# A delta-rule recurrence followed by an MLP: six-chunk key and query rings, a new load order, Newton key norms and a folded beta

## The chip, the cores and the metric

The kernel runs on 1 core of one Trainium2 chip. The metric is the device time of one execution in microseconds, the median over the runs of the kernel. A profile is one execution; its span is the time from the first to the last instruction of the core.

## What is computed

```python
def _attn_ref(q, k, v, beta):           # q, k, v: (4, 8, 768, 48); beta: (4, 8, 768)
    k_n = k / (np.linalg.norm(k, axis=-1, keepdims=True) + 1e-06)
    state = np.zeros((B, H, D, D))
    for t in range(S):
        y[:, :, t] = einsum('bhd,bhde->bhe', q[:, :, t], state)
        v_old = einsum('bhde,bhd->bhe', state, k_n[:, :, t])
        state = state + beta_t * einsum('bhd,bhe->bhde', k_n[:, :, t], v[:, :, t] - v_old)

def reference(...):                      # y as (3072, 384) rows x
    return gelu_tanh(x @ w_in) @ w_out   # w_in (384, 2048), w_out (2048, 384)
```

## The kernel before, in words

The sequence of 768 steps is cut into 12 chunks of C = 64 steps, for 32 heads held as 16 pairs (two heads of a pair on the two partition halves). A chunk goes through four stages.

- `prep(c)`: keys, queries and values come from DRAM by `load` (L522), two DMAs each, one for each half: 64 partitions x 16 pairs x 48 float32, 196,608 bytes a DMA. The key norms: squares `sq` on POOL or ACT, their sums `ss` (a DVE reduce, L613), the root `sr` (ACT Sqrt for chunks 0 to 2, for the later nine a POOL power with exponent 0.5, L330), an added 1e-6 (L622) and a reciprocal `rn` (L624) on DVE. Then `Kn = kf * rn` (POOL) and `Qn` (a cast), both bfloat16, and their transposes into `KQT`: on PE for chunks 0 to 2, by DMA transposes on the SP queue (L353) for the later ones. `kf`, `qf`, `vf` are rings of three buffers, `Kn` and `KQT` rings of RB = 4, indexed by chunk.
- `blocks(u)`: chunks are taken in units, [0], [1,2], [3,4], ..., [9,10], [11]. For a unit the 16x16 diagonal blocks of all its triangular systems are solved at once: matmuls of `own(u)` fill PSUM, a DVE 32x32 transpose makes `Tt` (L740), a product with `bM` makes `Yf`, then 14 pairs of small elementwise steps `tmp`, `Yf` run on POOL (on DVE for unit 0), and `XW[1]` (POOL, times minus beta) and `XW[0]` (ACT, a copy) go back to PE. All POOL work stands in one in-order queue, with the weight loads that POOL issues.
- `inverse(c, hs)`: from the solved blocks the whole 64x64 inverse `TT` of the chunk, by DVE products with masks (`WB` and `DI`, 128x1024 from PSUM, L785; `ET`; three `TT` steps) between PE products; `gram(c, g)` gives `G` and the masked `DT`.
- `state(c)`: the serial chain over chunks. `R = v - K S` (DVE), PE product with `TT`, `U = beta * (...)` (DVE, a product with `bcol`), PE product with `Kn`, `S = S + ...` (DVE), and the chunk's output `x` (ACT). The product of `U` and `Kn` is the last reader of `Kn`.

`mlp(t)` follows for tiles of one or two chunks, [0], [1,2], ..., [9,10], [11]: `x` is rearranged by six small DMAs on the SP queue, 16 groups of three matmuls `ps<-x,W` each followed by a Gelu on ACT into `gT`, then groups of eight matmuls `ps<-W,gT`, a copy `osb` and a store.

What sets the order: `Plan` holds every operation with a cost, its dependencies and a priority; `schedule()` (L106) places them one after another, per engine the ready operation with the lowest priority among those that are not later than `NEAR` of that engine, and emits each engine's queue in that fixed order with semaphore waits. Priorities are `T(c) = 28 c`; `prep(c)` has T(c-1), the MLP T + 1000 so that it fills gaps, its x DMAs a very low value. Loads are a queue of their own in one respect: `gate()` (L519) makes each load wait for the landing of the load written two before it in the program (`bulk[-2]`), and W_in (`load_w1`, `load_w1x`, eight DMAs) and W_out (`load_w2`, four DMAs) take part in it, issued by POOL. An instruction that waits holds back everything behind it on its queue. The plan's costs are estimates written into the kernel (1.05 us of DMA time for one key, query or value DMA); the chip's times are in the trace.

The program order of the loads is kf0, beta, qf0, kf1, qf1, vf0, W_in, kf2, qf2, vf1, W_out, vf2, then from iteration c = 1 on kf, qf and vf of chunk c + 2, each followed by `prep(c + 2)`:

```python
for c in range(NCH):
    if c + 2 < NCH:
        if c > 0:
            load("kf", c + 2, T(c - 1))
            load("qf", c + 2, T(c - 1))
        load("vf", c + 2, T(c - 1))
        prep(c + 2)
    u, sl = unit_of(c)
    if c == UNITS[u][0]:
        hs = blocks(u)
        ...
    state(c)
```

Of the kernel before, what the change touches and what calls it, by code (L numbers as in the profile page):

```python
# [376 lines left out]
def bass_deltanet__then__act_gelu_tanh_kernel(  # L377
# [25 lines left out]
    with nc.allow_non_contiguous_dma("head rows"), nc.allow_low_precision("bf16 matmuls"):  # L403
# [194 lines left out]

        def prep(c):
            s, i, j = c % RL, c % RB, c % 2  # L600
            pr = T(c, -STEP)
# [13 lines left out]
            ssn = [f"ss{j}{n}" for n in range(len(parts))]  # L615
            if c < NPE:
                op({"act": 0.24}, {"act": f_act(sr[j][:, :], ss[j][:, :], ACT.Sqrt)},
                   reads=ssn, writes=[f"sr{j}"], prio=pr)
            else:
                op({"pool": 2.95}, {"pool": f_tt(sr[j][:, :], ss[j][:, :], half[:, :], ALU.pow)},  # L620
                   reads=ssn + ["half"], writes=[f"sr{j}"], prio=pr)
            op({"dve": 0.1}, {"dve": lambda e: e.tensor_scalar(ss[j][:, :], sr[j][:, :], 1e-6, None, op0=ALU.add)},  # L622
               reads=[f"sr{j}"], writes=ssn, prio=pr)
            op({"dve": 0.25}, {"dve": lambda e: e.reciprocal(rn[j][:, :], ss[j][:, :])},  # L624
               reads=ssn, writes=[f"rn{j}"], prio=pr)
# [415 lines left out]
```

## Time and profile before

| | |
|---|---|
| median of 3 runs | 319.52 us (318.8 to 319.82) |
| the profiled execution | 316.87 us, its span 315.1 us |
| mean granted clock of PE over the span | 0.836 |
| PE busy | 240.2 us (76%) |
| DVE busy | 159.9 us (51%) |
| POOL busy | 139.8 us (44%) |
| ACT busy | 123.5 us (39%) |

PE is TensorE's matmuls, PEld its weight loads, DVE VectorE, ACT ScalarE, POOL GpSimd, SP the queue that issues most DMAs. In lines of the trace, `L330 POOL TENSOR_TENSOR sr<-ss,half 128x16` is an operation at line 330 (a helper's line, so tiles name the operation) that writes `sr` from `ss` and `half`; in square brackets, or behind a bar, stands the idle time before it and what ended it.

### The profile page before, as it was taken

What the parts mean: (1) busy time and instruction counts of PE and PEld (TensorE: products, weight loads), DVE (VectorE), ACT (ScalarE), POOL (GpSimd) and SP (SyncE); (2) the same over time, 40 slices, a digit from 0 to 9 for tenths busy, and PEclk for the clock granted to TensorE, in tenths of its full rate; (3) what the DMA queues carried; (4) which work ended last, traced back from release to release, by engine and by line L of the source; (5) the groups of instructions that cost most, each with busy time, mean ns of one, the idle gap of its engine ahead of it and who ended that gap; (6) DMA issues with size and microseconds to landing.
All of it is one profiled execution on the core that took longest, in us unless ns stands there. A gap on an engine that the chain in (4) does not pass through costs nothing.

```text
span 315.1 us, 13554 instructions
## 1 busy us (share of the span) xinstructions
PE 240.2 (76%) x6289; PEld 153.0 (49%) x6310; DVE 159.9 (51%) x250; ACT 123.5 (39%) x209; POOL 139.8 (44%) x246
## 2 busy tenths in 40 slices
PE   1714671779746869974897985899897999989995
PEld 1513660346644315664754553346665556455662
DVE  5799650119765212988633652347775545252111
ACT  3622460642213464221263742473122752166240
POOL 4580368572555499940103794995100006810000
PEclk9955555779755799985587999799998899999999
DMA  7999895999991985103299849800351000200112
GB/s 126 149 151 127 124 142 94 160 147 158 146 127 24 151 117 111 54 29 57 57 165 128 158 70 151 180 2 4 46 121 42 3 4 27 89 4 2 58 50 50
DMA packets 102808, 28.40 MB, mean 90 GB/s; under 512 B 96768, under 2 KB 102368, under 8 KB 102752
## 3 DMA queue, kind: packets, MB, share of 16 engines
q1 hardware_dynamic: 100128, 24.39, 48.0%
q0 software_dynamic: 2624, 3.15, 7.1%
q8 instruction: 49, 0.80, 1.1%
q14 instruction: 7, 0.06, 0.1%
HBM read 20.64 MB, written 4.72 MB: 80 GB/s over the span
## 4 chain that ended last, share of the span: by engine, by line
PE 38%; DMA 25%; SPq 14%; DVE 7%; ACT 6%; POOL 5%; issue 5%
PE ps L346 38%; DMA qf<-in_q_dram 14%; SPq L354 11%; DMA kf<-in_k_dram 3%; DMA W<-in_moe_w_out_dram 3%; DMA W<-in_moe_w_in_dram 3%; SPq L353 3%; POOL Yf L330 2%; DVE DI L785 2%; POOL tmp L330 2%; ACT gT L339 2%; ACT x L339 1%; DVE TT L330 1%; DVE U L330 1%; DVE R L330 1%
## 5 line engine op out<-in xcount | busy, mean ns | idle before, releaser
L346 PE MATMUL ps<-x,W 128*128 128x512 bf16 (+1 forms) x315 | 74.4, 379 | 18.7 <-DMA x<-x 9.7
L339 ACT ACTIVATE gT<-ps 128x512 bf16<-128x512 f32 (+1 forms) x112 | 58.2, 535 | 56.2 <-PE ps L346 54.7
L346 PE MATMUL ps<-W,gT 128*128 128x384 bf16 x384 | 69.4, 333 | 2.0 <-ACT gT L339 2.0
L346 PEld LDWEIGHTS ps<-x,W 128*128 128x128 bf16 x336 | 29.2, 104 | 51.8 <-ACT gT L339 18.9
L346 PEld LDWEIGHTS ps<-W,gT 128*128 128x128 bf16 x384 | 36.0, 99 | 26.0 <-ACT gT L339 2.6
L330 POOL TENSOR_TENSOR sr<-ss,half 128x16 f32<-128x16 f32 x9 | 26.2, 2912 | 30.8 <-DVE ss L613 30.8
L330 DVE TENSOR_TENSOR TT<-ps,DI 128x768 bf16<-128x768 f32 (+2 forms) x36 | 24.2, 688 | 18.4 <-PE ps L346 18.3
L613 DVE TENSOR_REDUCE ss<-sq 128x16 f32<-128x768 f32 (+1 forms) x13 | 11.5, 888 | 39.9 <-ACT sq L339 39.5
L330 POOL TENSOR_TENSOR Yf<-Yf,tmp 128x28 f32<-128x28 f32 (+6 forms) x84 | 28.8, 349 | 4.0
L346 PE MATMUL ps<-KQT 48*32 48x32 bf16 (+1 forms) x1280 | 22.5, 214 | 10.2 <-DMA KQT<-Kn 5.0
L330 POOL TENSOR_TENSOR tmp<-Yf 128x28 f32<-128x28 f32 (+6 forms) x84 | 27.8, 338 | 4.2
L330 POOL TENSOR_TENSOR Kn<-kf,rn 128x768 bf16<-128x768 f32 (+1 forms) x12 | 17.1, 1423 | 26.5 <-PE ps L346 22.8
L330 POOL TENSOR_TENSOR Yf<-Tt,bM 128x512 f32<-128x512 f32 x6 | 7.7, 1281 | 40.9 <-DVE Tt L740 40.9
L339 ACT ACTIVATE x<-ps 128x1024 bf16<-128x1024 f32 x12 | 12.3, 1024 | 31.8 <-PE ps L346 31.5
L346 PEld LDWEIGHTS ps<-KQT 48*32 48x32 bf16 (+1 forms) x1280 | 16.7, 106 | 16.1 <-DMA KQT<-Kn 5.9
L335 DVE COPY osb<-ps 128x384 f32<-128x384 f32 x16 | 8.9, 557 | 27.2 <-PE ps L346 26.9
L694 DVE TENSOR_TENSOR DT<-ps,mD 128x512 bf16<-128x512 f32 x24 | 16.3, 687 | 12.7 <-ACT G L339 12.3
L339 ACT ACTIVATE G<-ps 128x512 bf16<-128x512 f32 x24 | 13.9, 593 | 18.2 <-PE ps L346 18.0
L785 DVE TENSOR_TENSOR DI<-ps,mB 128x1024 bf16<-128x1024 f32 x12 | 14.6, 1219 | 11.2 <-PE ps L346 10.1
L346 PE MATMUL ps<-TT,ET 64*64 64x32 bf16 (+1 forms) x768 | 18.2, 184 | 2.5 <-DVE TT L330 1.8
L346 PEld LDWEIGHTS ps<-TT,ET 64*64 64x64 bf16 x768 | 16.2, 120 | 7.7 <-DVE TT L330 3.6
L785 DVE TENSOR_TENSOR WB<-ps,mB 128x1024 bf16<-128x1024 f32 x12 | 14.6, 1220 | 5.2 <-PE ps L346 5.2
(83 smaller groups left out, 285.8 us busy)
## 6 DMA issues: line engine op xcount, KB each, us to landing
kf<-in_k_dram SPq DMA_DIRECT2D x24, 192.0 KB, 4.8
qf<-in_q_dram SPq DMA_DIRECT2D x24, 192.0 KB, 4.8
vf<-in_v_dram SPq DMA_DIRECT2D x24, 192.0 KB, 4.4
out_dram<-osb SPq DMA_DIRECT2D x20, 192.0 KB, 2.0
W<-in_moe_w_in_dram POOLq DMA_DIRECT2D x8, 192.0 KB, 4.2
W<-in_moe_w_out_dram POOLq DMA_DIRECT2D x4, 384.0 KB, 5.3
out_dram<-osb SPq DMA_DIRECT2D x8, 96.0 KB, 2.3
x<-x SPq DMA_DIRECT2D x30, 16.0 KB, 1.9
```

The source lines that it names most:

```text
L330: return lambda e: e.tensor_tensor(out() if callable(out) else out, a() if callable(a) else a, b() if callable(b) else b, op)
L335: return lambda e: e.tensor_copy(out, a() if callable(a) else a)
L339: return lambda e: e.activation(out, a() if callable(a) else a, func)
L346: ins = t.matmul(out, lhsT, rhs, start=st, stop=sp_, skip_group_check=skip)
L353: return lambda e: e.dma_start_transpose(out, a)
L354: return lambda e: e.dma_start(out, a)
L613: op({"dve": 0.95 * w}, {"dve": lambda e, u=u: e.tensor_reduce(ss[j][:, u], sq[:, u, :], AX.X, ALU.add)}, reads=[f"sq{n}"], writes=[f"ss{j ...
L694: op(d_ps(512), {"dve": lambda e: e.tensor_tensor(pv(DTb[r_][:, ps_, :]), gview(1)(), mD[:, :].unsqueeze(1).unsqueeze(1).to_broadcast([128 ...
L785: op(d_ps(1024), {"dve": lambda e: e.tensor_tensor(dst.rearrange("q p (b j) -> q p b j", j=16), cmp_(w).unsqueeze(2).to_broadcast([128, NP ...
```

## The change

- Rings: RB goes from 4 to 6, so `Kn` and `KQT` hold six chunks. The raw rings `kf`, `qf`, `vf` stay at three.
- Loads: kf2 moves ahead of qf1, qf2 ahead of vf0 and W_in; kf3, qf3, kf4, qf4 come before W_out; vf2 after it. In the loop the key and query loads are five chunks ahead, `prep` three chunks ahead, the value load three chunks ahead and behind `state(c)`. Preps 1 and 2, and `own` and `blocks` of unit 1, get early priorities (-25.7, -25.4, -22.5, -22).
- Norms: for chunks 3 on the POOL power goes. The two chunks of a unit are normed together on DVE, from an integer estimate of the reciprocal root and three Newton steps: 13 DVE instructions on at most 128x32 for a unit (1 + 3 x 3 + 2 + a reciprocal). `Kn` of a unit's first chunk therefore waits for the keys of its second.
- Beta: `XW[0]` is multiplied by minus beta (POOL, on DVE for unit 0) in place of the ACT copy; `R` is now K S - v; `U` is then a plain copy from PSUM and goes from DVE to ACT.
- `DI` and `WB` shrink from 64 to 48 columns, so their products are 128x768. `gT` becomes a ring of 24 buffers in place of two sets of 16. The early PE transposes and Gram products may use all eight PSUM banks; the Gram product waits for `own` of its unit. `NEAR` of DVE and POOL becomes 0.1.

```diff
-NEAR = {"pe": 0.3, "dve": 0.05, "act": 0.05, "pool": 0.0, "sp": 0.0}
+NEAR = {"pe": 0.3, "dve": 0.1, "act": 0.05, "pool": 0.1, "sp": 0.0}
-        RL, RB, RT = 3, 4, 3
+        RL, RB, RT = 3, 6, 3
...
-        load("qf", 1, -66)
+        load("kf", 2, -66)
+        load("qf", 1, -65)
...
+            def norms(e, x, y):
+                return op({"dve": 0.17}, {"dve": e}, reads=x, writes=y, prio=pr)
...
+            elif c == UNITS[unit_of(c)[0]][-1]:
+                pair = UNITS[unit_of(c)[0]]
...
+                norms(lambda e: e.tensor_scalar(y_.bitcast(I32), s_.bitcast(I32), -0.5, 1597463007.0, op0=ALU.mult,
+                                                op1=ALU.add), sn_, yn_)
+                for _ in range(3):
+                    norms(f_tt(a_, y_, s_, ALU.mult), sn_ + yn_, ["nw"])
+                    norms(lambda e: e.scalar_tensor_tensor(a_, a_, -0.5, y_, ALU.mult, ALU.mult), yn_ + ["nw"], ["nw"])
+                    norms(lambda e: e.scalar_tensor_tensor(y_, a_, 1.5, y_, ALU.add, ALU.mult), yn_ + ["nw"], yn_)
+                norms(f_tt(a_, y_, s_, ALU.mult), sn_ + yn_, ["nw"])
+                norms(lambda e: e.tensor_scalar(a_, a_, 1e-6, None, op0=ALU.add), ["nw"], ["nw"])
+                op({"dve": 0.25}, {"dve": lambda e: e.reciprocal(rn2[:, z, :], a_)},
...
-                op({"pool": 2.95}, {"pool": f_tt(sr[j][:, :], ss[j][:, :], half[:, :], ALU.pow)},
...
-            op({"act": 0.65}, {"act": f_act(XW[j][0].rearrange("q c b r -> q b c r"), Y[:, :, :, :])},
+            fb = f_tt(XW[j][0].rearrange("q c b r -> q b c r"), Y[:, :, :, :],
+                      bt.unsqueeze(3).to_broadcast([128, 2, 16, 16]), ALU.mult)
+            op({"dve": 0.75} if u == 0 else {"pool": 1.5}, {"dve": fb, "pool": fb},
...
-            op(d_ps(NP * D), {"dve": f_tt(U[:, :, 0:D].rearrange("q (b m) d -> q b m d", b=2),
...
+            op(d_act(NP * D), {"act": f_act(uo, ui)}, reads=[h2] + [f"Uz{j2}"], writes=[f"U{j2}"], prio=pr)
...
+        load("qf", 2, -64)
+        load("vf", 0, -38)
         prep(0)
         prep(1)
-        load("vf", 0, -38)
...
-        load("kf", 2, -26)
-        load("qf", 2, -25)
+        prep(2)
         load("vf", 1, -24)
+        load("kf", 3, -27)
+        load("qf", 3, -26)
+        load("kf", 4, -25)
+        load("qf", 4, -24)
...
+        load("vf", 2, -15)
         for c in range(NCH):
-            if c + 2 < NCH:
-                if c > 0:
-                    load("kf", c + 2, T(c - 1))
-                    load("qf", c + 2, T(c - 1))
-                load("vf", c + 2, T(c - 1))
-                prep(c + 2)
+            if c + 3 < NCH:
+                prep(c + 3)
+            if c + 5 < NCH:
+                load("kf", c + 5, T(c - 1))
+                load("qf", c + 5, T(c - 1))
...
             state(c)
+            if c + 3 < NCH:
+                load("vf", c + 3, T(c - 1))
```

## Rows read from the trace of the kernel before

**Rows 1.** The page's 40 equal slices of the span, tenths, PE and its granted clock.
```profile
PE   1714671779746869974897985899897999989995
...
PEclk9955555779755799985587999799998899999999
```

**Rows 2.** Busy time by stretch: PE, PEld, DVE, ACT, POOL (instructions); clock, DMA share, GB/s.
```profile
5.00:45.00 40.00, 21.45 (x773) 18.01 (x777) 30.26 (x62) 17.33 (x25) 18.68 (x23) 0.65 0.96 142
54.00:103.00 49.00, 35.38 (x1072) 24.24 (x1074) 25.46 (x36) 17.62 (x35) 26.53 (x27) 0.67 0.93 127
103.00:134.00 31.00, 26.67 (x398) 13.33 (x398) 12.67 (x16) 14.63 (x25) 26.63 (x57) 0.95 0.71 107
134.00:160.00 26.00, 18.71 (x799) 15.31 (x800) 17.98 (x23) 5.86 (x9) 5.14 (x7) 0.62 0.34 60
160.00:200.00 40.00, 32.15 (x882) 18.97 (x883) 18.96 (x26) 18.36 (x30) 22.22 (x28) 0.93 0.89 138
200.00:300.00 100.00, 93.61 (x2253) 55.46 (x2264) 47.77 (x59) 43.43 (x77) 30.00 (x74) 0.98 0.15 39
```

**Rows 3.** Timeline of PE (start, duration): first MLP matmuls of tiles 0 and 1.
```profile
54.03 4.05 PE L346 MATMUL ps<-x,W 128*128 128x256 bf16 x18 [8.12 <-DMA x<-x]
...
103.25 2.34 PE L346 MATMUL ps<-x,W 128*128 128x512 bf16 x5 [0.33 <-issue]
```

**Rows 4.** Timeline of POOL: unit 1's solve and what interrupts it.
```profile
35.27 0.80 POOL L354 DMA_DIRECT2D W<-in_moe_w_out_dram  x1 [11.74 <-DMA qf<-in_q_dram]
...
42.29 1.27 POOL L330 TENSOR_TENSOR Yf<-Tt,bM 128x512 f32<-128x512 f32 x1 [1.10 <-DVE Tt L740]
...
59.76 2.94 POOL L330 TENSOR_TENSOR sr<-ss,half 128x16 f32<-128x16 f32 x1 [3.69 <-DVE ss L613]
...
65.34 1.48 POOL L330 TENSOR_TENSOR XW<-Yf,nbT 128x512 bf16<-128x512 f32 x1
```

**Rows 5.** Timeline of the SP queue: loads of qf1 and kf2.
```profile
9.25 1.31 SPq L354 DMA_DIRECT2D qf<-in_q_dram  x2
...
24.80 3.73 SPq L354 DMA_DIRECT2D kf<-in_k_dram  x2
```

**Rows 6.** Timeline of POOL: first and last operation of unit 6's solve (29 instructions between).
```profile
262.06 1.28 POOL L330 TENSOR_TENSOR Yf<-Tt,bM 128x512 f32<-128x512 f32 x1 [35.83 <-DVE Tt L740]
...
275.40 1.49 POOL L330 TENSOR_TENSOR XW<-Yf,nbT 128x512 bf16<-128x512 f32 x1
```

**Rows 7.** Waits by engine: us in total, times, longest.
```profile
ACT gT L339 <- PE ps L346: 54.7, 50, 7.5
...
POOL Kn L330 <- PE ps L346: 22.8, 5, 8.3
```

**Rows 8.** Groups of instructions by form: busy us, mean ns, idle before them.
```profile
L330 POOL TENSOR_TENSOR sr<-ss,half 128x16 f32<-128x16 f32 x9 | 26.2, 2912 | 30.8 <-DVE ss L613 30.8
...
L785 DVE TENSOR_TENSOR DI<-ps,mB 128x1024 bf16<-128x1024 f32 x12 | 14.6, 1219 | 11.2 <-PE ps L346 10.1 <-ACT TT L791 1.1
...
L330 DVE TENSOR_TENSOR U<-ps,bpad 128x768 bf16<-128x768 f32 x12 | 11.4, 952 | 11.0 <-PE ps L346 10.9
...
L330 DVE TENSOR_TENSOR ET<-ps,mE 128x768 bf16<-128x768 f32 x12 | 11.4, 951 | 2.6 <-PE ps L346 2.6
...
L330 POOL TENSOR_TENSOR XW<-Yf,nbT 128x512 bf16<-128x512 f32 x6 | 9.0, 1501 | 0.3
...
L339 ACT ACTIVATE S<-ps 128x768 bf16<-128x768 f32 x1 | 0.8, 811 | 0.2 <-PE ps L346 0.2
```

**Rows 9.** Timeline of DVE: small steps of unit 0's solve, both inputs in SBUF.
```profile
20.12 2.05 DVE L330 TENSOR_TENSOR tmp<-Yf 128x88 f32<-128x88 f32 x1
...
27.74 0.21 DVE L330 TENSOR_TENSOR tmp<-Yf 128x28 f32<-128x28 f32 x1
27.98 0.21 DVE L330 TENSOR_TENSOR Yf<-Yf,tmp 128x28 f32<-128x28 f32 x1
```

**Rows 10.** Timeline of POOL beside the first of rows 9.
```profile
20.57 1.49 POOL L330 TENSOR_TENSOR Kn<-kf,rn 128x768 bf16<-128x768 f32 x1
```

More of the change, by code (lines that the diff above doesn't have):

```diff
@@ L453, in bass_deltanet__then__act_gelu_tanh_kernel @@
         W2 = sb("W2", [128, FC, DM], BF16)
-        gT = [sb(f"gT{i}", [128, FC, 512], BF16) for i in range(2)]
+        NG = 24
+        gT = [sb(f"gT{i}", [128, 512], BF16) for i in range(NG)]
         NOSB = 4
@@ L597, in kts, with unit_of @@
             return [f"T0{c % RB}_{x}" for x in ((0, 1) if g is None else (g,))]
+        def unit_of(c):
+            return (c + 1) // 2, (c + 1) % 2
+        UNITS = [[c for c in (2 * u - 1, 2 * u) if 0 <= c < NCH] for u in range(NU)]
         def prep(c):
             s, i, j = c % RL, c % RB, c % 2
-            pr = T(c, -STEP)
+            pr = T(c, -STEP) if c in (0, 3) or c > 3 else -26 + 0.3 * c
             kn = [f"kf{s}_0", f"kf{s}_1"]
@@ L618, in prep @@
                    reads=ssn, writes=[f"sr{j}"], prio=pr)
-            else:
-                op({"pool": 2.95}, {"pool": f_tt(sr[j][:, :], ss[j][:, :], half[:, :], ALU.pow)},
[L621 to L625, printed above, removed]
+                norms(lambda e: e.tensor_scalar(sr[j][:, :], sr[j][:, :], 1e-6, None, op0=ALU.add), [f"sr{j}"], [f"sr{j}"])
@@ L626, in prep, with prep2 @@
+            for d in ([c] if c < NPE else UNITS[unit_of(c)[0]]):
+                prep2(d)
+        def prep2(c):
+            s, i, j = c % RL, c % RB, c % 2
+            pr = T(c, -STEP) if c in (0, 3) or c > 3 else -26 + 0.3 * c
+            kn = [f"kf{s}_0", f"kf{s}_1"]
+            qn = [f"qf{s}_0", f"qf{s}_1"]
+            parts = [slice(0, 8), slice(8, 16)] if c == 0 else [slice(0, NP)]
             for n, u in enumerate(parts):
@@ L659, in prep @@
                        writes=tn[kk] if np_ == 1 else [tn[kk][n]], prio=pr + 0.2 + 0.1 * kk)
-        def unit_of(c):
-            return (c + 1) // 2, (c + 1) % 2
-        UNITS = [[c for c in (2 * u - 1, 2 * u) if 0 <= c < NCH] for u in range(NU)]
         def pv(t):
@@ L823, in inverse @@
                 cols = slice(16 * k, 64)
-                op({"pe": 0.52}, {"pe": prod(hk, ET[e_], src[:, :, cols], n, per)}, nm=32, reads=sn + [f"ET{e_}"], free=[f"TT{r_}b"],
+                op({"pe": 0.52}, {"pe": prod(hk, ET[e_], src[:, :, 16 * k - off:64 - off], n, per)}, nm=32, reads=sn + [f"ET{e_}"], free=[f"TT{r_}b"],
                    writes=[hk], alloc=[(hk, NP // per)], prio=pr + 0.3 + 0.2 * k)
-                op(d_ps(16 * n), {"dve": f_tt(two(TT[r_][:, :, cols], per), view(hk, n, per), two(DI[r_][:, :, cols], per),
+                op(d_ps(16 * n), {"dve": f_tt(two(TT[r_][:, :, cols], per), view(hk, n, per), two(DI[r_][:, :, 16 * k - 16:48], per),
                                               ALU.add)},
                    reads=[hk, f"DI{r_}"], writes=[f"TT{r_}b"], prio=pr + 0.4 + 0.2 * k)
-                src, sn = TT[r_], [f"TT{r_}b"]
+                src, off, sn = TT[r_], 0, [f"TT{r_}b"]
         def state(c):
@@ L936, in mlp @@
             pr = T(chunks[-1] + 1, 1000)
-            s = t % 2
+            gs = [(16 * t + fc) % NG for fc in range(FC)]
             xs = x4[t % NX]
@@ L963, in m2 @@
                     def m2(h=h, u=u, part=part):
[L964 removed]
+                        return [(bank(h)[:, 0:DM], gT[gs[fc]][:, 128 * u:128 * u + 128], W2[:, fc, :], fc == 0,
                                  fc == FC - 1, False) for fc in range(8 * part, 8 * part + 8)]
                     op({"pe": 1.31}, {"pe": f_mms(m2)}, nm=8, mode="m", bk=mo,
[L967 removed]
+                       reads=[f"gT{gs[fc]}" for fc in range(8 * part, 8 * part + 8)] + W2N + ([h] if part else []),
                        writes=[h], alloc=[] if part else [(h, 1)], prio=pr + 40 + u * 4 + part * 2)
```

60 lines of the change are left out of this document (32 added, 28 removed).

## The prediction

> **What bounds the kernel now.** I read the page's slices first. PE is nearly full over the last third of the span and full of holes before that, at a low granted clock for most of slices 3 to 14 and again at 19 and 20 [rows 1]. So no engine bounds the whole; the kernel is PE-bound late and waits for something early. The stretches say how much: from 54 to 103 us PE is busy 35.4 of 49 us at a clock of 0.67, from 134 to 160 18.7 of 26 at 0.62, from 160 to 200 32.2 of 40, but from 200 to 300 93.6 of 100 at 0.98 [rows 2]. The MLP is the filler that would close the holes, and it can't start before its input: tile 0 begins at 54.0 us, tile 1, which needs chunks 1 and 2, only at 103.3 [rows 3]. What is late for tile 1 is the solve of unit 1 on POOL, from 42.3 to 65.34 + 1.48 = 66.8 us, with a weight issue that held POOL 11.7 us before it and a hole that ends in a root for chunk 3 within it [rows 4]. And behind that stands the load of kf2, issued at 24.8 us, 15.5 us after qf1 [rows 5]. That order of loads is what the change turns round.
>
> **The change part by part.** All times are those of the profiled execution (span 315.1).
>
> *Unit 1 starts earlier.* kf2 takes the place of qf1, 9.25 in place of 24.80 [rows 5]. With the same distance from its issue to the first step of the solve, 42.3 - 24.8 = 17.5 us [rows 4, 5], the solve starts at 26.8. Against that, kf2 and qf2 now stand ahead of vf0 and W_in: 2 x 2 x 196,608 bytes at the 142 GB/s of that stretch [rows 2] are 5.5 us of loading, and DVE, busy 30.3 of 40 us there [rows 2], is shared with unit 0's solve. So 26.8 to 32.3; I take 29, 13 us gained.
>
> *The solve itself.* It took 24.5 us. Unit 6, undisturbed, took 275.40 + 1.49 - 262.06 = 14.8 [rows 6]. The changed one adds a second `XW` on POOL, 1.5 us [rows 8], in place of an ACT copy beside it. No root interrupts it now. W_out's four issues (0.8 each [rows 4]) stay on POOL, and four loads (kf3 to qf4) now stand ahead of them in the gate's chain, 11 us more at 142 GB/s: a POOL that reaches such an issue early waits as it did for 11.7 us. Lower bound 14.8 + 1.5 = 16.3, upper bound 24.5 + 1.5 + 11; I take 21, nearer the undisturbed row since POOL's plan loses the roots. XW is then ready at 50, 17 us before 66.8; bounds 46 to 62.
>
> *From there to tile 1.* 103.3 - 66.8 = 36.5 us for two inverses and two states [rows 3, 4]. Some of it was waiting for loads of later chunks on DVE's and POOL's in-order queues; I take 4 off (0 to 9). Tile 1 begins at 82, bounds 75 to 98. A step later: the six x DMAs of each tile and the DMA transposes stand on SP behind key and query loads that are now five chunks ahead and may wait there for a free raw buffer (three, as before). I price that at nothing, because the x DMAs have a priority below all loads; if that cover fails it is one load's gate, 2.8 us a tile.
>
> *From tile 1 to the end.* Before, 315.1 - 103.3 = 211.9 us. PE idles 4.3, 7.3, 7.9 and 6.4 us in the four stretches from 103 to 300 [rows 2]. With chunks 3 and 4 prepared some 17 us earlier, the hole of 134 to 160 should close (5 of 7.3, and 3 more because its 18.7 us of work ran at 0.62). The six-deep ring removes POOL's waits for a free `Kn`, 22.8 us in 5 waits [rows 7]; the work queued behind them is the next unit's keys and solve, and I count 5 us of PE's idle time in 103 to 134 and 160 to 200 for it. Together -13, bounds -3 to -20.
>
> *Norms.* Nine roots of 2.91 us, 26.2 us, leave POOL [rows 8]; five units x 13 DVE instructions come. Dependent small steps start 0.24 us apart [rows 9], so a unit costs 3.1 us, all five 15.6; some 4 us of the old adds and reciprocals go. That is the lower end. The upper: the same step with two inputs in SBUF took 2.05 us at 20.12 where others of its kind took 0.21, and ended with a 1.49 us POOL operation [rows 9, 10]. Ten of the 13 have two SBUF inputs. Beside a solve, whose steps are about 0.35 us, that is up to 3.1 + 10 x 0.35 = 6.6 us a unit, 33 in all, and more beside long POOL operations. The plan counts 2.3 a unit. PE has MLP work queued at most of these points, so I put +4 on the path (0 to +25). The Trainium skill (SBUF — State Buffer, section "Who interferes with whom") says that a DVE instruction with two SBUF inputs and a GpSimd one that reads SBUF exclude each other for a whole instruction, whichever came first; that speaks against norms on DVE, rows 9 and 10 agree, and by it alone the term would lie at its upper end.
>
> *U on ACT, narrower masks.* `U` took 0.95 us on DVE; ACT's copy of the same shape took 0.81 [rows 8], so 12 x 0.14 = 1.7 us shorter on the state chain. But ACT is in order, and its Gelus wait for PE 54.7 us in 50 waits, 1.1 each [rows 7]: a `U` behind one waits with it, up to 12 x 1.1 = 13 us. I take +2. The Trainium skill (ScalarE: Activation LUTs, section "Rules for kernel authors") wants plain arithmetic on VectorE rather than ScalarE; by the row ACT is the quicker here, by the rule the copy would gain nothing and the term would be +3.7. `DI` and `WB` become 768 wide, 1.22 to the 0.95 of `ET` [rows 8], 24 x 0.27 = 6.5 us of DVE, off the path mostly; the one `XW` of unit 0 costs DVE about 1 us and these shorter masks give 0.5 back. The `gT` ring, the banks and `NEAR` I take at nothing: Gelus of the next tile may run 8 ahead in place of 16, and PE has products of `W` to do then; if that cover goes it is one Gelu's wait per tile, 1.1 us x 6.
>
> **Sum.** 82 + 211.9 - 13 + 4 + 2 = 287 us of span, 28 less than 315.1. Launch and end add 316.87 - 315.1 = 1.8, and the median of the runs stands 0.8% above the profiled execution (319.52 / 316.87): 288.8 x 1.0084 = 291 us. With the front's bounds and the later terms as taken the span is 75 + 205 to 98 + 205, measured 284 to 307. All terms at their ends at once would give 75 + 192 = 267 to 98 + 247 = 345; the upper end is the slower rival's.
>
> **The rivals.** *The front moves little.* The plan believes in faster loads than the chip gives, and POOL's and SP's queues are in order: unit 1's solve starts early, but stands at W_out's gates until about 60, so tile 1 begins near 96, 7 us earlier; with the later terms 96 + 205 = 301, or 305 measured. For it: the 11.7 us wait of rows 4. Against: kf2 alone is 15.5 us earlier. *PE full to the end.* From 54 to 300 us PE worked 206.6 us [rows 2]; of the 19 that its work at 0.67 and 0.62 would give back at full clock I count 12; at the density of the stretch from 200 to 300 that is 194.6 / 0.936 = 208 in place of 246, 38 us less, 281 measured, and lower if tile 0 starts before 54. It needs everything to work. *Slower: norms locked against POOL.* Each of the five Newton chains falls beside a POOL solve, takes 6.6 us or more (rows 9 at 2.05), and `R`, `S` and the masks queue behind it while PE's fixed order waits. It decides when over 28 us of the five chains are exposed, 5.6 a unit: with 37 of them the end is at 287 - 4 + 37 = 320, or 325 measured. For it rows 9 and 10, against it that PE has filler and that POOL loses 26 us. *It does nothing:* priorities, not the order written, decide the queues, and the plan might issue kf2 late all the same; 319.5.
>
> **How the numbers follow.** My forecast, tile 1 20 us earlier and a denser end, 0.60, likeliest 291, own range 282 to 303. The front moving little 0.18 (303 to 312). PE full 0.07 (270 to 282). Nothing 0.05. Slower 0.10. A measurement of this kernel tells 0.3% from no change. Faster 0.60 + 0.18 + 0.07 = 0.85, same 0.05, slower 0.10. A range of 275 to 312 leaves out the last two and the best part of the full PE, some 0.18.
>
> **What would show it.** Right: kf2's load near 9 us, unit 1's first `Yf` near 29 and last `XW` near 50; tile 1's first product near 82; no wait of `Kn` for PE; the stretch 134 to 160 over 0.85 busy at a clock near 1; POOL busy some 17 us less (26.2 less 9.0 for the new `XW`). Newton steps of 0.24 us on average would show the lock unimportant, over 0.4 important. Wrong: tile 1 after 95; W_out issues with long waits on POOL inside the solve; `U` on ACT starting over 1 us after its product ended; a tile 0 later than 58, through DVE or the six x DMAs.

## The result and the profile after

The changed kernel takes 305.13 us (median of 4 runs: 301.43, 302.68, 307.58 and 308.28) beside 319.16 for the kernel before (318.54 to 319.82), 4.4% less. The ratio is 0.9464, interval 0.9414 to 0.9514; ratios here are of the runs within 1.5% of the fastest of their kernel and session, which leaves out the two upper ones here and four profiled runs of the table below (after measured again, plan told the DMA times, early front, old loads), whose rows are read for places and order and not for the last microseconds. The profiled execution took 302.68 us with a span of 300.9, 14.2 less than before. Measured once more in another session (below), the same kernel ran 307.78 to 314.86, ratio 0.9704, interval 0.963 to 0.9779. So the gain is 3% to 5%. The two upper runs of the first session are as long as the lower ones of the second: this kernel varies from run to run by more than one interval tells, and no single part can be priced finer than that.

The page's slices, beside [rows 1]:

```profile
PE   1564266578698877993699997989899899999994
...
PEclk9999999999979999796899998699999999999999
```

From slice 10 to 17 PE is more even (8, 6, 9, 8, 8, 7, 7, 9 where it had a 4 and two 6), but slices 19 and 20 are a hole still, 3 and 6, as 18 and 19 were before, 7 and 4. The clock row looks full for the first third; the last section says why that is worth little.

Busy time by stretch (PE, PEld, DVE, ACT, POOL; clock, DMA share, GB/s), beside [rows 2]:

```profile
5.00:45.00 40.00, 19.04 (x630) 15.15 (x630) 34.42 (x68) 13.95 (x21) 28.63 (x45) 1.00 0.95 143
54.00:103.00 49.00, 38.17 (x1074) 25.37 (x1070) 24.99 (x49) 24.00 (x44) 23.79 (x41) 0.97 0.96 145
...
134.00:160.00 26.00, 18.11 (x469) 9.11 (x469) 17.27 (x40) 13.14 (x24) 21.86 (x56) 0.87 0.79 125
160.00:200.00 40.00, 36.97 (x1180) 23.57 (x1181) 20.65 (x28) 14.29 (x22) 10.46 (x12) 0.91 0.42 75
200.00:300.00 100.00, 93.11 (x1943) 54.94 (x1937) 35.21 (x47) 41.38 (x75) 27.01 (x64) 1.00 0.11 33
```

The stretch from 134 to 160, which the prediction wanted filled, is as empty as before: 18.1 of 26 us. What grew is 160 to 200, 37.0 for 32.2, and 54 to 103, 38.2 for 35.4. DVE was the busiest engine from 5 to 45 us already, with 30.3 of 40, and has 34.4 there now.

The timeline of PE, first products of tiles 0, 1 and 2, beside [rows 3]:

```profile
66.28 1.46 PE L347 MATMUL ps<-x,W 128*128 128x256 bf16 x6
...
91.91 3.08 PE L347 MATMUL ps<-x,W 128*128 128x512 bf16 x12
...
142.58 3.29 PE L347 MATMUL ps<-x,W 128*128 128x512 bf16 x9 [0.40 <-DMA x<-x]
```

and of tile 2 in the kernel before:

```profile
157.07 2.34 PE L346 MATMUL ps<-x,W 128*128 128x512 bf16 x5 [0.40 <-DMA x<-x]
```

Tile 0 starts 12.3 us later, tile 1 11.3 earlier, tile 2 14.5 earlier. From there to the end are 158.3 us, and 158.0 before: **in this profile the whole gain stands at tile 2, and nothing is added behind it.** Two stretches cut at these points, before and then after, show why:

```profile
157.07:315.10 158.03, 139.97 (x3229) 82.65 (x3246) 69.03 (x90) 65.66 (x115) 52.22 (x101) 0.95 0.36 68
```

```profile
142.58:300.90 158.32, 144.53 (x3376) 85.06 (x3376) 68.19 (x102) 66.49 (x115) 52.25 (x112) 0.97 0.25 53
```

Behind tile 2 PE works 89% of the time before and 91% after, and it has 4.6 us more to do there. With 240.2 and 237.7 us of PE work in all, 100.2 us of it lay ahead of tile 2 before and 93.2 lie there now, so PE idles 49.4 us ahead of tile 2 where it idled 56.9, and 13.8 behind it where it idled 18.1. These 7.5 and 4.3 us, and 2.5 us less work, are the 14.2 us.

### The profile page after: what moved, and what is told of

It is laid out like the page before. It is cut to its first block, busy times and chain, and to the rows that moved or that the text cites. A ratio compares the mean times of both kernels' runs of the same rounds, so it can differ in the third digit from the quotient of the medians.

```text
span 300.9 us, 13620 instructions
## 1 busy us (share of the span) xinstructions
PE 237.7 (79%) x6310; PEld 150.3 (50%) x6310; DVE 159.1 (53%) x292; ACT 122.9 (41%) x207; POOL 127.9 (42%) x245
## 4 chain that ended last, share of the span: by engine, by line
PE 51%; DMA 20%; SPq 11%; DVE 7%; issue 4%; ACT 4%; POOL 3%; ACTq 0%
PE ps L347 50%; SPq L355 9%; DMA kf<-in_k_dram 9%; DMA W<-in_moe_w_in_dram 4%; DMA qf<-in_q_dram 4%; SPq L354 2%; DMA vf<-in_v_dram 2%; DMA BL<-in_beta_dram 1%; POOL sq L331 1%; DVE ss L618 1%; ACT gT L340 1%; ACT sq L340 1%; POOL Kn L331 1%; DVE TT L331 1%; POOL W L355 1%
## 5 line engine op out<-in xcount | busy, mean ns | idle before, releaser
L347 PE MATMUL ps<-x,W 128*128 128x512 bf16 (+1 forms) x336 | 76.8, 366 | 6.2 <-ACT gT L340 5.4
L347 PE MATMUL ps<-W,gT 128*128 128x384 bf16 x384 | 71.7, 337 | 2.3 <-ACT gT L340 2.3
L347 PEld LDWEIGHTS ps<-W,gT 128*128 128x128 bf16 x384 | 36.1, 100 | 26.3 <-issue 2.7
L331 DVE TENSOR_TENSOR TT<-ps,DI 128x768 bf16<-128x768 f32 (+2 forms) x36 | 24.6, 687 | 22.2 <-PE ps L347 21.8
L336 DVE COPY osb<-ps 128x384 f32<-128x384 f32 x18 | 10.0, 558 | 45.4 <-PE ps L347 45.4
L347 PE MATMUL ps<-KQT 48*32 48x32 bf16 (+1 forms) x1280 | 21.0, 206 | 15.2 <-DVE DT L719 4.9
L331 POOL TENSOR_TENSOR Yf<-Yf,tmp 128x28 f32<-128x28 f32 (+6 forms) x84 | 29.8, 355 | 6.6
L331 POOL TENSOR_TENSOR tmp<-Yf 128x28 f32<-128x28 f32 (+6 forms) x84 | 29.1, 346 | 6.6
L347 PEld LDWEIGHTS ps<-KQT 48*32 48x32 bf16 (+1 forms) x1280 | 15.7, 101 | 20.5 <-issue 6.5
L331 POOL TENSOR_TENSOR Kn<-kf,rn 128x768 bf16<-128x768 f32 (+1 forms) x12 | 17.3, 1448 | 19.2 <-DVE rn L643 19.2
L340 ACT ACTIVATE U<-ps 128x768 bf16<-128x768 f32 x12 | 9.7, 809 | 37.0 <-PE ps L347 36.9
L340 ACT ACTIVATE G<-ps 128x512 bf16<-128x512 f32 x24 | 13.7, 594 | 13.8 <-PE ps L347 13.8
L618 DVE TENSOR_REDUCE ss<-sq 128x16 f32<-128x768 f32 (+1 forms) x13 | 11.4, 884 | 13.8 <-ACT sq L340 10.5
L331 DVE TENSOR_TENSOR S<-ps,S 128x768 bf16<-128x768 f32 x10 | 9.6, 955 | 15.5 <-PE ps L347 15.4
L347 PE MATMUL ps<-identB,XW 32*32 32x32 bf16 x896 | 11.2, 204 | 5.8 <-DVE DT L719 4.3
L340 ACT ACTIVATE Qn<-qf 128x768 bf16<-128x768 f32 x10 | 8.4, 842 | 17.5 <-DMA qf<-in_q_dram 17.5
```

What stands on the lines that cost most here:

```text
L331: return lambda e: e.tensor_tensor(out() if callable(out) else out, a() if callable(a) else a, b() if callable(b) else b, op)
L336: return lambda e: e.tensor_copy(out, a() if callable(a) else a)
L340: return lambda e: e.activation(out, a() if callable(a) else a, func)
L347: ins = t.matmul(out, lhsT, rhs, start=st, stop=sp_, skip_group_check=skip)
L618: op({"dve": 0.95 * w}, {"dve": lambda e, u=u: e.tensor_reduce(ss[j][:, u], sq[:, u, :], AX.X, ALU.add)}, reads=[f"sq{n}"], writes=[f"ss{j ...
```

## The experiments

First product of each tile in the profiled run of each kernel, in us, with the ratio to the kernel before of the same session:

| kernel | tile 1 | tile 2 | tile 3 | span | ratio (interval) |
|---|---|---|---|---|---|
| before | 103.25 | 157.07 | 201.09 | 315.1 | 1 |
| after | 91.91 | 142.58 | 187.63 | 300.9 | 0.9464 (0.9414 to 0.9514) |
| after, measured again | 95.41 | 149.50 | 194.16 | 313.1 | 0.9704 (0.963 to 0.9779) |
| before + rings, masks | 105.15 | 148.87 | 191.34 | 308.6 | 0.9807 (0.9764 to 0.9849) |
| after with old norms and beta | 90.31 | 141.54 | 201.97 | 310.8 | 0.9751 (0.9687 to 0.9815) |
| after with POOL's power | 92.41 | 144.06 | 194.86 | 304.0 | 0.9609 (0.9568 to 0.9649) |
| after with old beta | 93.17 | 142.25 | 191.36 | 304.4 | 0.959 (0.9529 to 0.965) |
| after, two reduces held back | 88.79 | 144.77 | 188.53 | 306.2 | 0.9666 (0.9562 to 0.9769) |
| after, plan told the DMA times | 94.84 | 142.20 | 191.22 | 307.6 | 0.958 (0.9474 to 0.9685) |
| after with old `NEAR` | 96.64 | 147.12 | 189.86 | 304.3 | 0.9679 (0.9586 to 0.9773) |
| before + early front | 92.03 | 157.60 | 201.47 | 322.8 | 1.0079 (1.0021 to 1.0137) |
| after, key ring of four | 91.15 | 139.88 | 185.67 | 303.9 | 0.9622 (0.9566 to 0.9678) |
| after with old loads | 100.06 | 144.91 | 199.37 | 315.4 | 0.9688 (0.9624 to 0.9751) |
| after, other latency in the plan | 99.49 | 147.23 | 189.06 | 301.6 | 0.9566 (0.9501 to 0.9632) |

From the start of tile 2 to the end these profiles take 154.4 us (other latency) to 170.5 (old loads). So an early tile 2 doesn't bring the end with it by itself: with old norms and beta it starts at 141.5 and the span is still 310.8.

**Rings and masks alone.** The kernel before with

```diff
-        RL, RB, RT = 3, 4, 3
+        RL, RB, RT = 3, 6, 3
...
-        DI = [sb(f"DI{i}", [128, NP, C], BF16) for i in range(RT)]
-        WB = [sb(f"WB{i}", [128, NP, C], BF16) for i in range(2)]
+        DI = [sb(f"DI{i}", [128, NP, 48], BF16) for i in range(RT)]
+        WB = [sb(f"WB{i}", [128, NP, 48], BF16) for i in range(2)]
...
-        gT = [sb(f"gT{i}", [128, FC, 512], BF16) for i in range(2)]
+        NG = 24
+        gT = [sb(f"gT{i}", [128, 512], BF16) for i in range(NG)]
...
```

> The kernel before with the rings alone: Kn and KQT of six chunks, the gT ring of 24 and the 48-column masks that make room for it; loads, norms and beta as before. Front theory (the gain is unit 1's earlier keys): kf2 is still issued near 25 us, so tile 1 begins at 101 to 104 us and the time is 315 to 320. Ring theory (the gain is POOL's 22.8 us of waits for a free Kn): those waits go and the time falls to 305 to 310.

Measured 312.06 us, 0.9807, between the two cases written down. Its tile 1 is no earlier than before, 105.15:

```profile
105.15 7.85 PE L346 MATMUL ps<-x,W 128*128 128x512 bf16 x24 [3.53 <-DMA x<-x]
...
148.87 2.74 PE L346 MATMUL ps<-x,W 128*128 128x512 bf16 x6 [0.41 <-DMA x<-x]
```

but tile 2 is 8.2 us earlier, and 6.5 of it reach the end. The waits of `Kn` for PE of [rows 7] are gone. So without any earlier front the rings and masks together bring about 2%; that those waits were what it hung on is not shown by this run, and the run with the key ring of four below speaks against it.

**The front alone.** The kernel before with the early loads of kf2 and qf2 and the early due times of prep 1, prep 2 and unit 1:

```diff
-        load("qf", 1, -66)
+        load("kf", 2, -66)
+        load("qf", 1, -65)
+        load("qf", 2, -64)
...
-            pr = T(cs[0], -STEP + 6)
+            pr = T(cs[0], -STEP + 6) if u != 1 else -22.5
...
```

> The kernel before with the front of the change alone: kf2 and qf2 loaded ahead, prep 2, own and blocks of unit 1 early; rings of four, later loads, norms and beta as before. Front theory: unit 1's solve ends near 48, tile 1 begins at 85 to 93, time 304 to 310. Giving-back theory (the middle, from tile 2 on, is held by keys, roots and Kn and eats an earlier front): tile 1 as early, but tile 2 no earlier than 150 and time 312 to 319.

Measured 321.83 us, 1.0079, so a little slower, and above both cases written down. Its timeline of PE has tile 1 where the changed kernel has it, and tile 2 where the kernel before has it:

```profile
92.03 1.46 PE L346 MATMUL ps<-x,W 128*128 128x512 bf16 x6 [1.40 <-DMA x<-x]
...
157.60 2.52 PE L346 MATMUL ps<-x,W 128*128 128x512 bf16 x6
```

and its stretch from 134 to 160 is still a hole at a low clock:

```profile
134.00:160.00 26.00, 20.55 (x783) 17.16 (x778) 18.71 (x23) 5.20 (x8) 6.62 (x11) 0.50 0.30 55
```

This is the plainest result of the study: 11 us won at tile 1 are given back whole before tile 2. Chunk 3's `x` is evicted at 141.9 us as before (140.28), where the changed kernel has it at 121.6; what holds chunk 3 here is not shown. What the prediction called the main gain is none by itself.

**Rings and loads, without norms and beta.** The changed kernel with the POOL power for chunks from 3 on, the ACT copy for `XW[0]` and the product with beta on DVE for `U`:

```diff
-                norms(lambda e: e.tensor_scalar(y_.bitcast(I32), s_.bitcast(I32), -0.5, 1597463007.0, op0=ALU.mult,
-                                                op1=ALU.add), sn_, yn_)
...
+                op({"pool": 2.95}, {"pool": f_tt(sr[j][:, :], ss[j][:, :], half[:, :], ALU.pow)},
...
-            op(d_act(NP * D), {"act": f_act(uo, ui)}, reads=[h2] + [f"Uz{j2}"], writes=[f"U{j2}"], prio=pr)
+            op(d_ps(NP * D), {"dve": f_tt(U[:, :, 0:D].rearrange("q (b m) d -> q b m d", b=2),
...
```

> The changed kernel with the old norms (POOL power, chunk by chunk) and the old beta (product in U on DVE, ACT copy of XW): rings, loads, priorities alone. Front theory: most of the 17 us stays, tile 1 begins at 88 to 96, time 302 to 308. Norm theory (the gain is POOL and DVE freed of roots and of U): 313 to 320.

Measured 311.07 us, 0.9751, between the two cases written down. Tiles 1 and 2 are where the changed kernel has them (90.3, 141.5), but tile 3 comes at 202.0, 14.3 us later than there: all that tile 2 had won is lost again on the way to tile 3. Ahead of that stretch and in it, pairs of roots hold POOL for 5.8 us at a time:

```profile
102.25 5.78 POOL L331 TENSOR_TENSOR sr<-ss,half 128x16 f32<-128x16 f32 x2
...
166.00 5.78 POOL L331 TENSOR_TENSOR sr<-ss,half 128x16 f32<-128x16 f32 x2
```

The roots alone don't make that loss: the next run has such pairs at the same places (102.5 and 165.2) and its tile 3 at 194.9.

**Old norms alone.** The same edit to the norms, beta as changed.

> The changed kernel with the POOL power for the norms, everything else changed. Front theory: within 4 us of the changed kernel, 299 to 306, since the Newton chains take DVE 14 us and free POOL 26. Norm theory: the roots stand in POOL's queue before the next solves again, 8 us or more slower, 310 to 316.

Measured 305.74 us, 0.9609, as the front theory has it.

**Old beta alone.** The same edit to `XW`, `R` and `U`, Newton steps as changed.

> The changed kernel with beta back in U (DVE product, ACT copy of XW[0]), everything else changed. Front theory: within 4 us of the changed kernel, 299 to 306. Norm and beta theory: U back on DVE behind Newton steps and masks costs 0.15 to 0.5 us in each of 12 chunks on the state chain plus DVE's queue, 6 us or more slower, 308 to 314.

Measured 307.85 us (303.6 to 309.84), 0.959, the median just outside both cases. With either of the two put back alone, tile 3 comes at 194.9 or 191.4, not at 202.0. Against the first session of the changed kernel each would seem to be worth 1.5%; against the second, neither anything. What stands without choosing a session is that these two, run in one session with the kernel that lacks both, are better than it, by some 1.5% and with intervals apart (up to 0.9649 and 0.965, from 0.9687); with old beta this rests on two of four runs, for the other two, 309.52 and 309.84, are as long as those of the kernel that lacks both (307.92 to 312.52).

**Two reduces held back.** In the changed kernel DVE stands before the reduce of kf4's squares while chunk 0's chain waits behind it (the chain of waits, below). Here these reduces depend on chunk 0's `U`:

```diff
+                if c in (3, 4):
+                    guarded.append(red)
...
+            if c == 0:
+                for g_ in guarded:
+                    g_.deps.add(uop.idx)
```

> The changed kernel with one edge more: the DVE sums of squares of chunks 3 and 4 wait for chunk 0's U, so that DVE's fixed order can't hold chunk 0's last TT behind keys that land at 47 us. Theory of the late keys (chunk 0's chain lost its lead in DVE's queue): chunk 0's x at 51 to 53 in place of 55.5, tile 0 begins at 61 to 63, tile 1 at 87 to 90, time 297 to 300. Rival (PE's own order and the low clock hold tile 0, or what follows is bound elsewhere): x moves, the time stays within 2 us of 302.

Measured 307.07 us, 0.9666, outside both cases. Tile 1 comes at 88.8, 3.1 us earlier, tile 2 at 144.8, 2.2 later. But chunk 0's `x` hardly moved: 55.2 us in place of 55.5. DVE did finish chunk 0's last inverse at 46.6 in place of 49.3, and then PE's fixed order had unit 1's `XW` product next, which waited for POOL, so that `U` came only 0.7 us earlier. Of tile 1's 3.1 us, 1.7 are shorter pauses of PE ahead of tile 0, 0.44 and 1.03 us for 1.29 and 1.84 (last section). So the theory of the late keys fell: the wait that the chain of waits names is not what makes chunk 0 late.

**The plan told the measured DMA times.**

```diff
-                   reads=after, writes=[f"{nm}{s}_{a}"], prio=pr, dma=f"d_{nm}{c}", bw=1.05)
+                   reads=after, writes=[f"{nm}{s}_{a}"], prio=pr, dma=f"d_{nm}{c}", bw=1.4)
```

and likewise 1.1 to 1.4 for W_in and 2.2 to 2.8 for W_out.

> The changed kernel with the plan's DMA costs raised to the measured rate (1.4 in place of 1.05 us for a key, query or value DMA, 1.4 for 1.1 and 2.8 for 2.2 for the weights). Late-keys theory: fewer waits of DVE, ACT and POOL behind late loads, 296 to 300. Rival: the plan's order differs at random only, 300 to 308.

Measured 305.64 us, 0.958, tile 2 at 142.2: in the rival's range, and within what the same kernel varies by.

**The old `NEAR`.**

```diff
-NEAR = {"pe": 0.3, "dve": 0.1, "act": 0.05, "pool": 0.1, "sp": 0.0}
+NEAR = {"pe": 0.3, "dve": 0.05, "act": 0.05, "pool": 0.0, "sp": 0.0}
```

> The changed kernel with NEAR of DVE and POOL as before (0.05 and 0). Front theory: the window matters little, 300 to 305. Order theory (a good part of the gain is that the plan happens on a good order in the middle): a change this small moves the time by more than 3 us, 305 to 311.

Measured 307.42 us, 0.9679: in the range of the order theory, but also within what the unaltered kernel varies by (301.43 to 314.86), so it decides nothing.

**The changed kernel again.** No edit; one session for this and the three that follow.

> The changed kernel once more, beside the three runs below. If the 0.946 of its first measurement holds from session to session, 299 to 304 us (0.945 to 0.952 of before). If the other variants stood beside a slower session, 305 to 308 us, and then the 1.5% that norms and beta seemed to bring is no more than that.

Measured 310.11 us (307.78, 308.73, 311.5 and 314.86), 0.9704: slower than both cases that were written down. The first session had 301.43, 302.68, 307.58 and 308.28; its lower pair is not seen again here, its upper pair is. Something of the difference between the two profiles (302.68 and 314.86 us) can be read, in places and not in sums. The waits of PE, first and second time (us in total, times, longest):

```profile
PE ps L347 <- issue: 13.2, 14, 1.8
```

```profile
PE ps L347 <- issue: 23.8, 34, 3.2
```

Some of the second sum are waits of 0.16 or 0.33 us ahead of a group of matmuls that lacks one or two, so records that are missing and no waits. Leaving out all up to 0.34, the sums are 12.5 us in 12 waits and 20.4 in 16. The long ones fall at the same instructions each time. Timeline of PE, first and second time:

```profile
59.10 0.57 PE L347 MATMUL ps<-S,KQT 48*64 48x48 bf16 x25 [1.29 <-issue]
...
63.75 1.73 PE L347 MATMUL ps<-TT,ET 64*64 64x16 bf16 x58 [1.84 <-issue]
```

```profile
61.45 0.56 PE L347 MATMUL ps<-S,KQT 48*64 48x48 bf16 x25 [3.23 <-issue]
...
66.92 1.73 PE L347 MATMUL ps<-TT,ET 64*64 64x16 bf16 x58 [2.67 <-issue]
```

A group of 32 like products stops after the seventh, in the middle, with no engine or load shown that it waits for, 1.29 us the first time and 3.23 the second; the last section reads from the trace what ends these waits. Of the 3.2 us by which tile 0 is later the second time (69.45 for 66.28) the first two of these waits are 1.94 + 0.83 = 2.8.

**The key ring of four.** The changed kernel with

```diff
-        RL, RB, RT = 3, 6, 3
+        RL, RB, RT = 3, 4, 3
```

> The changed kernel with the key ring put back to four buffers; all else as changed. Theory that the rings make room for the front: chunk 4's and 5's keys then wait for chunk 0's and 1's, tile 2 begins after 148 us instead of 142.6, and the end is 308 to 314 us. Rival, that a kernel whose states are no longer late can do with four buffers: tile 2 within 2 us of 142.6 and 301 to 306 us.

Measured 306.39 us, 0.9622, tile 2 at 139.88. The waits of `Kn` for PE are back, and longer than in [rows 7]:

```profile
POOL Kn L331 <- PE ps L347: 42.4, 5, 20.6
```

Yet tile 2 is no later and the kernel no slower than the changed one beside it (0.9704). The theory that the six key buffers make room for the front fell: given the rest of the change, four are enough, and POOL's waits for a free `Kn` cost nothing that the end shows. What the rings brought in the run of rings and masks therefore came from there being no other relief, or from the `gT` ring and the narrow masks, which that run had too; the two weren't separated.

**The old loads.** The changed kernel with the loads, the lookahead and unit 1's due times of before:

```diff
-        load("kf", 2, -66)
-        load("qf", 1, -65)
+        load("qf", 1, -66)
...
-            if c + 3 < NCH:
-                prep(c + 3)
-            if c + 5 < NCH:
-                load("kf", c + 5, T(c - 1))
-                load("qf", c + 5, T(c - 1))
+            if c + 2 < NCH:
+                if c > 0:
+                    load("kf", c + 2, T(c - 1))
+                    load("qf", c + 2, T(c - 1))
+                load("vf", c + 2, T(c - 1))
+                prep(c + 2)
...
```

> The changed kernel with the loads, the lookahead of two chunks and the due times of unit 1 put back; rings, Newton steps and beta stay as changed. Theory that the new load order sets the front: tile 1 begins at 101 to 106 us instead of 92. If the rings then pass the 11 us on to the end, 308 to 314 us; if what bounds the middle is the states and not the front, as the run with the front alone says, 302 to 307 us.

Measured 309.33 us, 0.9688, no worse than the changed kernel beside it (0.9704). The time lies in the first of the two ranges written down, but so does that of the changed kernel measured beside it (310.11), and tile 2's place speaks for the second. Tile 1 begins at 100.06, near the old 103.25, and tile 2 at 144.91 all the same:

```profile
100.06 2.34 PE L347 MATMUL ps<-x,W 128*128 128x512 bf16 x5 [0.33 <-issue]
...
144.91 2.34 PE L347 MATMUL ps<-x,W 128*128 128x512 bf16 x5 [0.90 <-DMA x<-x]
```

It is the counterpart of the run with the front alone: an early tile 1 without the rest gives nothing, and the rest without an early tile 1 gives 3%.

**Another order of the same instructions.** The changed kernel with

```diff
-LAT = {"pe": 0.22, "dve": 0.06, "act": 0.06, "pool": 0.08, "sp": 0.0}
+LAT = {"pe": 0.22, "dve": 0.07, "act": 0.06, "pool": 0.08, "sp": 0.0}
```

> The changed kernel with one constant of its planner altered (VectorE's assumed latency 0.07 for 0.06 us), which deals out another order of the same instructions and nothing else. If the order is worth little, within 1% of the changed kernel, 300 to 306 us. If single parts can't be told from the order that the planner happens to deal, 1% to 3% off it to either side: 296 to 299 us or 307 to 312 us.

Measured 304.53 us (303.33 to 307.35), 0.9566, where the changed kernel beside it ran 307.78 to 314.86. A constant that only deals another order of the same instructions seems to be worth about as much as a whole part of the change. But the changed kernel in its own order ran 301.43 to 308.28 in the first session, which takes in all of these runs, so that what the order is worth is not shown apart from how the kernel varies. It is the best version of that session, and no version here is shown to beat the changed kernel.

**What the runs settle.** That the gain is 3% to 5%; that an early tile 1 is neither needed for it nor enough; that of key ring, load order, norms and beta each can be undone alone and leave 3% to 4%, so that their shares don't add up. What stays open is which of the parts common to all the faster variants (the `gT` ring, the 48-column masks, the banks) carries most; whether those that can be undone stand in for each other, as norms and beta seem to do, or are worth nothing each; and how much of the 1.5% of norms and beta is the plan's order.

## Why the prediction was right and wrong

The time came out 14 us above the 291 of the forecast: 2 us above the forecast's own range (282 to 303), inside the wide one (275 to 312), which takes in the rival of the front that moves little. The direction was right, and the gain half of the 28 us foreseen. Of the 13.9 us by which the span passed its 287, 9.9 stand ahead of tile 1 and 4.0 behind it. That a measurement of this kernel tells 0.3% from no change was wrong as well: four runs of the changed kernel lie 2.3% apart. By its steps:

**Unit 1 starts earlier: right.** The SP queue issues kf2 with kf1, and kf3 and kf4 later, beside [rows 5]:

```profile
5.86 4.87 SPq L355 DMA_DIRECT2D kf<-in_k_dram  x4
...
35.95 1.31 SPq L355 DMA_DIRECT2D kf<-in_k_dram  x2
...
40.89 1.52 SPq L355 DMA_DIRECT2D kf<-in_k_dram  x2
```

**The solve: right.** POOL's timeline, beside [rows 4]:

```profile
31.72 1.28 POOL L331 TENSOR_TENSOR Yf<-Tt,bM 128x512 f32<-128x512 f32 x1 [0.95 <-DVE Tt L765]
...
46.02 2.49 POOL L331 TENSOR_TENSOR XW<-Yf,nbT 128x512 bf16<-128x512 f32 x2
48.46 1.66 POOL L355 DMA_DIRECT2D W<-in_moe_w_out_dram  x2
```

From 31.7 to 48.5 where 29 and 50 were foreseen; the solve took 16.8 us, near its lower bound, and the W_out issues stand behind it, not in it. So the rival of the front that moves little gave the span that was measured (301 us, and 300.9) by a mechanism that did not occur.

**From there to tile 1: the first term that failed.** 32.5 us were foreseen, 36.5 less 4; it took 91.9 - 48.5 = 43.4. Beside the 4 us that were not won, 2.6 more went into the two inverses and states (from the solve's end to chunk 2's eviction, 31.2 us for 28.6), and 4.4 more between that eviction and tile 1 (12.2 us for 7.8), where PE was still at work on a late tile 0. The step that failed is that chunk 0 was left out: the early front is paid for by it. The prediction named DVE's sharing with unit 0's solve, but put a price on it for unit 1 only, and its sign of being wrong, a tile 0 later than 58, came true with 66.3. Timeline of PE, the first product of unit 0's solved blocks, before and after:

```profile
29.09 1.89 PE L346 MATMUL ps<-identB,XW 32*32 32x32 bf16 x128 [3.14 <-ACT XW L339]
```

```profile
36.62 1.90 PE L347 MATMUL ps<-identB,XW 32*32 32x32 bf16 x128 [4.29 <-DVE DT L719]
```

So 7.5 of tile 0's 12.3 us are lost by there, 6.1 of them by the end of unit 0's solve on DVE (36.0 us for 29.8), which has the preps of chunks 1 and 2 in its order beside it. That the front does this, the runs show from both sides: the same product comes at 36.1 with the front alone, and at 29.2 with the old loads, whose tile 0 begins at 53.3. `U` of chunk 0 comes at 50.9 us, where it came at 42.1. The four loads that now stand ahead of W_out add little. The chain of waits, as far as it runs through this:

```profile
41.53 5.94 DMA kf<-in_k_dram
...
47.56 0.85 ACT sq L340
48.41 0.02 issue
48.43 0.95 DVE ss L618
49.39 0.34 DVE TT L331
```

The reduce for kf4, which nobody needs before chunk 4, stands in DVE's fixed order ahead of chunk 0's last inverse, and waits 3.0 us for a load; but with the two reduces held back `U` came only 0.7 us earlier. The states of chunks 1 and 2 did get the front's gain (x evicted at 70.8 and 79.7 for 85.8 and 95.4, 15 and 15.7 us earlier).

**The x DMAs priced at nothing: wrong at tile 2.** Chunk 4's state is evicted by 133.0 us, by ACT's timeline

```profile
132.00 1.00 ACT L340 ACTIVATE x<-ps 128x1024 bf16<-128x1024 f32 x1
```

but SP has a transposing load, a query load, another transposing load and a store ahead of tile 2's x:

```profile
127.39 4.06 SPq L354 DMA_TRANSPOSE KQT<-Kn  x2
131.50 2.56 SPq L355 DMA_DIRECT2D qf<-in_q_dram  x2
134.10 2.05 SPq L354 DMA_TRANSPOSE KQT<-Qn  x1
136.20 0.58 SPq L355 DMA_DIRECT2D out_dram<-osb  x1
136.83 4.51 SPq L355 DMA_DIRECT2D x<-x  x6
```

They start 3.8 us after the eviction; before, at 151.11, 0.03 us after it. The price named in the prediction for this cover going was 2.8 us a tile; it is 3.8 at tile 2, 0.9 at tile 1 and nothing at tile 3. PE's hole from 136.2 to 140.7, which ends at a `DT` of DVE, lies just there, and tile 2's first product, in the timeline shown first, still waits 0.40 us for x. What tile 2 would gain from x ahead of those loads wasn't tried.

**From tile 1 to the end: the second term that failed, mis-sized.** -13 was foreseen, with norms and `U` at +6: 205 us. It took 209.0, where it took 211.9 before: -3.1 to tile 2 (50.7 for 53.8), +0.3 from there, so -3 in all in place of -7. The hole of 134 to 160, worth 8 of the 13, didn't close: its waits are 4.5 us for a `DT` of DVE, 2.8 for Gelus and 0.4 for tile 2's x, and none for keys. And behind tile 2 PE is at 91%, so an earlier state has little to fill there. The waits of `Kn` for PE, worth 5, went as foreseen, but the run with the key ring of four has 42.4 us of them at no cost, so those 5 were not there to be won beside the rest of the change. The `gT` ring was put at nothing; the run of rings and masks, which has it, gained 6 us with tile 1 where it was, and what share is its own wasn't tried. Here POOL waits for the Newton steps instead (waits by engine, beside [rows 7]):

```profile
POOL Kn L331 <- DVE rn L643: 19.2, 3, 8.6
```

**Norms: the busy time right, at the lower end.** By form, busy us and mean ns, beside [rows 8]:

```profile
L331 DVE TENSOR_TENSOR nw<-sr,ss 128x32 f32<-128x32 f32 x16 | 3.6, 226 | 0.5
...
L640 DVE SCALAR_TENSOR_TENSOR sr<-nw,sr 128x32 f32<-128x32 f32 x12 | 2.7, 228 | 0.3
```

All 65 steps are 14.3 us of work, 0.22 each, against 15.6 (starts 0.24 apart) at the lower end and 33 at the upper. But they don't stand together: from its first step to its reciprocal a unit's chain takes 14.5, 4.8, 4.7, 9.5 and 21.0 us, with DVE's other work between, and POOL's 19.2 us above end with such reciprocals; what they cost at the end is not shown. Two of the five chains have no POOL operation beside them: those 27 steps take 0.20 us on average, the longest 0.35. The 38 beside a solve take 0.23, the longest 0.41 where the same kind takes 0.19 alone. The rule of the Trainium skill (SBUF — State Buffer, section "Who interferes with whom") put the term at its upper end; the trace agrees with it for single steps, which lost up to 0.2 us beside POOL steps, but over the three chains that is only some 1.4 us. One `Yf` step of unit 0's solve on DVE took 2.84 us where its neighbours took 0.23 to 0.25; a `Kn` product of POOL began 0.4 us behind its start, at 23.57, and took 1.49, and POOL's next operation was still running when the step ended:

```profile
22.86 0.25 DVE L331 TENSOR_TENSOR tmp<-Yf 128x88 f32<-128x88 f32 x1
23.15 2.84 DVE L331 TENSOR_TENSOR Yf<-Yf,tmp 128x88 f32<-128x88 f32 x1
```

So the rival of the locked norms had the right mechanism, but only three of its five chains fell beside a solve, and there the neighbours are 0.25 to 0.46 us long; it strikes harder in unit 0's solve, beside POOL's 1.49 us products. POOL's busy time fell by 11.9 us (139.8 to 127.9), not by 17.

**U on ACT: the +2 was nothing.** 12 copies of 809 ns, as the row for `S` said:

```profile
L340 ACT ACTIVATE U<-ps 128x768 bf16<-128x768 f32 x12 | 9.7, 809 | 37.0 <-PE ps L347 36.9
```

Eleven of them started 0.04 us after their product's end and one (chunk 4's) 0.79, none over 1. `DI` and `WB` at 952 and 956 ns are right. The rule of the Trainium skill (ScalarE: Activation LUTs, section "Rules for kernel authors") gives additions and products to VectorE and names no copy; carried over to this one, it would have gained nothing. The row of the trace has it 0.14 us shorter, so the measurement decides for ACT at this size.

**PE full to the end** needed the holes ahead of tile 2 closed; 49.4 us of idle time are left there.

## What to carry to other kernels

Ask of an early gain which later point it must reach, and measure that point: here tile 1 was moved by 8 and by 11 us without the end following. Ask also which work pays for it: here chunk 0 lost 9 us to the earlier unit 1. Where a stretch behind that point is over 90% busy, count nothing for what gets ready earlier in it. In a kernel whose queues are dealt by a planner, measure a mere reordering (one constant altered) and the same kernel in a second session before a part is priced at 1% or 2%.

## What the runs showed of the hardware

**PE stops inside groups of like products, and goes on 1.2 to 1.8 us after a block of instructions has landed.** The sum of such waits over 0.34 us is 8.4 us in the profile of before, 12.5 in that of after, 20.4 in that of after measured again, 12.4 to 24.5 in the other variants of it, 13.1 with rings and masks and 16.6 with the front alone. The page's list of DMA queues has one for instructions:

```profile
q8 instruction: 49, 0.80, 1.1%
```

Its 49 packets have 16,384 bytes each, and the trace holds the start and the end of each. The 12 waits of after end 1.25 to 1.71 us after the end of such a packet, the 16 of after measured again 1.20 to 1.66, and of the 167 in all 14 profiles 166 end 1.19 to 1.80 us after one, though a packet comes only every 6 us or so. So what PE waits for there is its instructions. The pause of 1.29 us in the middle of 32 products has its packet from 56.53 to 57.57 us and ends at 59.10; the second time the packet ran from 58.38 to 59.79, began only after PE had stopped, and the pause of 3.23 us ended at 61.45. The place is the program's; the length hangs on when the packet starts. Where the 16 DMA engines were less than 30% busy the waits are 1.0 us on average (55 of them), elsewhere 1.5 (112). That loads moved forward lengthen them is not shown: the run with the old loads has 15.1 us. How much of the difference between the two sessions they are stays open too, since the run with the old `NEAR` has 21.8 us of them in a span of 304.3.

**The granted clock of a stretch can say 1.00 while products run as long as at the lower level.** In the profile after, at a clock of 1.00 from 60 to 68 us, 32 products of 64x48 take 1.08 us; at 73.8 they take 0.69. Timeline of PE:

```profile
65.27 1.08 PE L347 MATMUL ps<-R,TT 64*64 64x48 bf16 x32
...
73.83 0.69 PE L347 MATMUL ps<-R,TT 64*64 64x48 bf16 x32
```

Tile 0's products do the same: six of 128x256 take 1.46 us at 66.3 and 0.83 at 70.9. Before, 32 products of 64x48 took 1.05 us at 32.9 and 35.0, where that column says 0.50 (30 to 38 us). So the lower of the two levels (1.2 GHz) seems to have been in force in both, and was entered in the column in one. The mean clock, 0.836 and 0.966, therefore tells of no gain of that size; the durations of a fixed shape tell more.
